# Second expert product with the weights stationary in five long lists, and a new way to preset the dispatch rows

## The chip, the cores and the metric

One core of one Trainium2 chip runs the whole program in one launch. The time is device microseconds (us) from the first to the last instruction of an execution. The kernel before takes 632.26 us, the median of 3 runs (632.22 to 633.16).

## What is computed

Three parts follow each other (reference, cut):

```python
# 1. attention: B=2, H=8, S=768, D=64, 16 clusters per head
mask = argmax(q_n @ c_n.T)[:, None] == argmax(k_n @ c_n.T)[None, :]
attn = softmax(where(mask, q @ k.T / 8, -1e9));  x = attn @ v      # 1536 tokens x 512
# 2. top-2 mixture of 8 experts, F=1024
out[tok] += w[tok] * (relu(x[tok] @ w1[e]) @ w2[e])                # per expert e
# 3. soft mixture: 8 experts x 4 slots, F=1024, softmax over tokens and over slots
```

## The kernel before, in words

**Attention.** The 16 heads are taken as 8 pairs p, each with two halves qh of the queries; I call the 16 steps h = 2p + qh *half-stages*. In one, TensorE (PE) computes six score tiles (`score`, L382 and L384), ScalarE (ACT) exponentiates them (L388), PE multiplies by v (`av`, L401), and GpSimd (POOL) adds up the exponentials (`add`, L418 and L421). Beside that PE finds the row maxima of the next half-stages (`munit`, L340, reduced by VectorE, DVE, L345 and L350). The finished maxima must become one row of the query operand (partition 96): `mfin` transposes them on DVE (L360) and writes the row with four DMAs (L363), except for the pairs in `TF`, where `mrow` does it with six small PE products (L371) and an ACT copy (L373). All loads go through one queue, SyncE's (SP), in the order of the program: for the next pair the values (`load_v`, L137) and the queries and keys (`load`, L128 and L129).

**Dispatch.** Each token's row (512 values and 4 of routing: expert, two weights, token number; `XR` = 516) is scattered to two of 3712 slots in DRAM (`xg`). Slots that stay empty must hold zeros and a token number that points to a row nobody reads (`TRASH` and above). `Dispatch.setup` (L498) makes constants on POOL and DVE at the end of half-stage 0 and presets the 4 routing columns of all slots with one DMA (L523); `fill` (L529) zeroes the other 512 columns of `xg`, and the sum of the experts `x2acc`, in 23 DMAs, four in each odd half-stage from h = 1.

**Experts.** The slots make ten jobs (lists) with 8 steps each, one step for 128 of the 1024 hidden units: two of 256 slots, six long ones of 448, 432, 408, 400, 392 and 384 used slots, and two of 240. Numbers are kept as the sum of a high and a low part (fp32r), so each product takes three matmuls. `first` (L1039) multiplies x by w1 with the weights stationary and the slots moving (L1054, 12 matmuls); ACT and DVE make the high and low part of the hidden row `H` (L1060, L1063). `second` (L1066) has it the other way round: H is stationary, 128 slots at a time, and the 512 columns of w2 move (L1095). A long list takes 9 such matmuls for its first 384 slots and, where there is a rest, 2 for the high and low part of the rest together: 11 of 512 columns, whatever the rest.

```python
for i, (a, x) in enumerate(((hi, XH), (hi, XL), (lo, XH))):     # first, four c each
    nc.tensor.matmul(ph[:, :u], a[:, 128 * c:128 * c + 128], x[:, c, :u], ...)
terms = [(py, HH[:, c], w, 0), (py, HH[:, c], v, 1), (py, HL[:, c], w, 2)]   # second
```

The order is written out: in step s come `first(s+1)`, `second(s)`, `split_hi(s+3)` on ACT (L952) and `split_lo(s+3)` on DVE (L959), which make the two parts of the weights in a ring of three, then pieces of the next list's x: `prep_t` (DVE transposes, L1009), `prep_h` (ACT), `prep_l` (POOL). After a list's last step `evac` weights the rows, and an indirect DMA of POOL adds them to `x2acc` (L1103). `xr` and `xT`, the two halves of one buffer, hold x before and after its transpose. `M2.load_w` loads the third part's weights, 2 MB at a time.

Of the kernel before, what the change touches and what calls it, by code (L numbers as in the profile page):

```python
# [472 lines left out]
class Dispatch:  # L473


    def __init__(self, tc, g, noise):
        self.tc, self.nc, self.g, self.noise_in = tc, tc.nc, g, noise
        xp = g.xp
        self.noise = xp.tile([128, NCK, E], F32, name="noise")
        self.z = g.place(DM)  # L480
        self.zm = g.place(NSL // 128, 4)
        g.xg = tc.dram_tile([NSL, XR], F32, name="xg")
# [15 lines left out]
    def setup(self):  # L498
# [16 lines left out]
        nc.gpsimd.tensor_tensor(self.lim, self.base, self.capm[:, None, :].to_broadcast([128, B, E]), op=OP.add)  # L515
        dv.tensor_scalar(self.lim[:, 1:, :NREG], self.lim[:, 1:, :NREG], float(LATE - RCAP), None, op0=OP.add)
# [10 lines left out]
        nc.gpsimd.tensor_copy(g.x[:, :, DM + 3], self.tok)  # L527

    def fill(self, i):  # L529

        nc, g = self.nc, self.g
        r = 2
        nx = NSL // 128
        for t, n in ((g.xg, nx), (g.x2, (NTOK + NTRASH) // 128)):
# [360 lines left out]
class MoE1:  # L895


    def __init__(self, tc, g, w12):
# [16 lines left out]
        self.wr, self.xr, self.xm, self.H, self.PH, self.PY = {}, {}, {}, {}, {}, {}  # L915
        self.scat = []
        self.spacer = mo.tile([1, 1], F32, name="spacer")
# [45 lines left out]
    def load_x(self, j):  # L963
# [7 lines left out]
        else:  # L971
            xg = lambda a, n, c: g.xg[r0 + a:r0 + a + n, c]
        xr, xT = self.XR[:, 0, x0:], self.XR[:, 1, x0:]
        for a in range(4):
# [49 lines left out]
    def prep_m(self, j):  # L1024

        nc, g = self.nc, self.g
        dv = nc.vector
        e, nb, xr, xT, xTv, mt, XH, XL, v = self.parts(j)
        del self.xr[j]
        k = mt.shape[1]  # L1030
        wt = g.mo0.tile([128, 4], F32, name="mwt", tag="mwt", bufs=2)[:, :k]
        di = g.mo0.tile([128, 4], U32, name="mdi", tag="mdi", bufs=2)[:, :k]
        dv.tensor_tensor(wt, mt[:, :, 1], mt[:, :, 2], op=OP.subtract)
        dv.scalar_tensor_tensor(wt, mt[:, :, 0], self.perm[:, j - NSRT:j - NSRT + 1] if e is None else float(e), wt, op0=OP.is_equal, op1=OP.mult)
        dv.tensor_tensor(wt, wt, mt[:, :, 2], op=OP.add)
        dv.tensor_copy(di, mt[:, :, 3])
        self.xm[j] = wt, di

    def first(self, s):  # L1039
# [17 lines left out]
        H = self.HT[:, s % 3]  # L1057
        m = n // 128 * 128
        HH, HL = H[:, :n], H[:, 2 * n - m:2 * n]
        nc.scalar.activation(HH[:, :u], ph[:, :u], AF.Relu)  # L1060
        for a, b, o in ((0, min(m, u), HL), (m, u, H[:, n:2 * n - m])):
            if a < b:
                nc.vector.scalar_tensor_tensor(o[:, :b - a], ph[:, a:b], 0.0, f32(HH)[:, a:b], op0=OP.max, op1=OP.subtract)  # L1063
        self.H[s] = HH, HL

    def second(self, s, ms=None):  # L1066
# [6 lines left out]
        hi, lo = self.ring[s]  # L1073
        last = j == len(self.jobs) - 1
        if f == NF - 1 and j not in self.Y:
            self.Y[j] = [self.mo.tile([128, DM], F32, name="y", tag="y", bufs=4) for i in range((n + 127) // 128)]
        nm = (n + 127) // 128
        for m in range(nm) if ms is None else ms:
# [7 lines left out]
            w, v = hi[:, 512:], lo[:, 512:]  # L1086
            if n - 128 * m >= 128:
                terms = [(py, HH[:, c], w, 0), (py, HH[:, c], v, 1), (py, HL[:, c], w, 2)]
            else:

                h = self.HT[:, s % 3, c.start:2 * n - c.start]
                o = py[:2 * (n - c.start)]
                terms = [(o, h, w, 0), (o, h, v, 2)]
            for o, x, y, i in terms:
                nc.tensor.matmul(o, x, y, start=(f == 0 and i == 0), stop=(f == NF - 1 and i == 2))  # L1095
            if f == NF - 1:
                for i in (m,) if last or m == nm - 1 and m % 2 == 0 else (m - 1, m) if m % 2 else ():
                    self.evac(j, i, self.PY[i])

    def add_rows(self, j, y, di, out):  # L1100
# [10 lines left out]
    def evac(self, j, m, py):  # L1111
# [3 lines left out]
        p = min(128, self.used[j] - 128 * m)  # L1115
        w = self.jobs[j][2] - 128 * m
# [3 lines left out]
        if w < 128:  # L1120
            nc.scalar.activation(yv, pv[w:w + p], AF.Copy, scale=wt[w:w + p, m:m + 1])
            for k in range(4):
                nc.vector.scalar_tensor_tensor(yv[:, k], pv[:p, k], wt[:p, m:m + 1],
                                               yv[:, k], op0=OP.mult, op1=OP.add)
        elif m % 2:
# [337 lines left out]
def body(tc, qk, q2, k2, v2, cent, wgn, noise, w12, phi, v12, out):  # L1463
    nc = tc.nc
    with ExitStack() as ctx:
# [103 lines left out]
        for n in range(1, NP):  # L1569
# [16 lines left out]
            at(post, 6 * h + (8 if n == 1 else 6), A.aql, n, 0)  # L1586
            at(post, 6 * h + 11, A.aql, n, 1)
            at(ends, h, A.load_v, n)
# [29 lines left out]
        for i in range(Dp.NFILL):  # L1618
            at(ends, 2 * (i // 4) + 1, Dp.fill, i)

# [85 lines left out]
        for h in range(2 * NP - 2):  # L1706
# [21 lines left out]
            for k in range(6):  # L1728
                A.av(p, 6 * qh + k)
                if s0 == 0 and k == 3:  # L1730
                    A.mrow(0, 1)
            gap(s0 + 5, 4)
            if s0 == 0:
                Dp.setup()
            run(ends, h)
# [49 lines left out]
        for s in range(ns):  # L1785
# [22 lines left out]
            if s == OV:  # L1808
                Dp.overflow(w12, lambda n: g.psum.tile([128, 512], F32, tag="mx", name=n, bufs=2))
                c_pre.close()  # L1810
                c_xp.close()
                M2.rooms(enter(c_w2, "m2w", side="right"), 6)
            q = s + 3
            soon = NREG * NF - 4 <= s < NREG * NF
# [5 lines left out]
            for fn, a in () if soon else prep.get(s, ()):  # L1820
                fn(*a)
            if s == 6:
                assert len(todo) <= 6
# [91 lines left out]
```

## Time and profile before

| | |
|---|---|
| median of 3 runs | 632.26 us |
| the profiled execution, its own time | 630.61 us |
| its span, first to last instruction | 628.8 us |
| PE busy | 605.9 us, 96% |
| DVE, ACT, POOL busy | 61%, 50%, 46% |
| granted PE clock | full in all 40 slices |

The profiled execution is 1.65 us below the median of the runs. A row of the timeline reads: start, duration, engine, line, operation, output<-inputs, shape, count, and in brackets the idle time before it with what ended it. A row of the chain of waits gives start, duration, engine, output and line; in it consecutive instructions of a line are one row.

### The profile page before, as it was taken

The numbers are of one execution on the slowest core, as the hardware profiler recorded it, in microseconds if no ns is written. First come the engines' busy times: TensorE is split into PE (matmuls) and PEld (weight loads), VectorE is DVE, ScalarE is ACT, GpSimd is POOL, SyncE is SP. The second block draws the span as 40 slices with busy tenths as digits, with TensorE's granted clock in tenths as the row PEclk, the third lists the DMA queues.
The fourth block names the chain that finished last, engine by engine and source line by source line (L and its number), as shares of the span: only waits on it lengthen the run. The fifth ranks groups of instructions, "written<-read, shape, count | busy, mean of one in ns | idle before, by whom it ended". The sixth has DMA issues, their size and how long they took to land. (4 is left out here: it accounts for less than half of the span.)

```text
span 628.8 us, 11424 instructions
## 1 busy us (share of the span) xinstructions
PE 605.9 (96%) x4169; PEld 472.5 (75%) x4169; DVE 385.0 (61%) x840; ACT 312.6 (50%) x444; POOL 287.1 (46%) x274
## 2 busy tenths in 40 slices
PE   8997999999999998999999999999999999988996
PEld 6665667666677667878888888888888888875544
DVE  6875667686776498757555445455544467646633
ACT  5857666676676661545344353444435445533002
POOL 3998777787989842642034241342513303120100
PEclk9999999999999999999999999999999999999999
DMA  8287474543446573897738559698794939988995
GB/s 327 68 188 211 182 267 169 212 151 124 142 178 211 203 208 124 281 237 194 168 100 181 164 203 254 233 299 311 234 334 140 235 128 342 296 255 302 427 388 201
DMA packets 62892, 139.50 MB, mean 222 GB/s; under 512 B 15280, under 2 KB 30832, under 8 KB 60784
## 3 DMA queue, kind: packets, MB, share of 16 engines
q1 hardware_dynamic: 56944, 125.31, 59.7%
q0 software_dynamic: 5888, 13.42, 9.9%
q8 instruction: 34, 0.56, 0.4%
q14 instruction: 26, 0.21, 0.1%
HBM read 108.18 MB, written 28.42 MB: 217 GB/s over the span
## 5 line engine op out<-in xcount | busy, mean ns | idle before, releaser
L1095 PE MATMUL py<-ring,H 128*128 128x512 f32 (+1 forms) x686 | 172.8, 396 | 1.2 <-DVE H L1063 1.2
L959 DVE TENSOR_TENSOR ring<-wr,ring 128x1024 fp32r<-128x1024 f32 (+1 forms) x77 | 95.0, 1235 | 103.6 <-ACT ring L952 103.5
L1095 PEld LDWEIGHTS py<-ring,H 128*128 128x128 f32 (+1 forms) x686 | 123.7, 184 | 28.4 <-DVE H L1063 2.5
L952 ACT ACTIVATE ring<-wr 128x1024 fp32r<-128x1024 f32 x77 | 81.6, 1061 | 92.0 <-PE py L1095 82.3
L1103 POOL DMA_INDIRECT x2acc<-y,mdi x31 | 50.4, 1625 | 103.5 <-ACT y L1128 97.7
L345 DVE TENSOR_REDUCE mp<-pmx 128x1 f32<-128x512 f32 x96 | 63.6, 683 | 15.8 <-PE pmx L340 15.4
L1060 ACT ACTIVATE H<-ph 128x256 fp32r<-128x256 f32 (+7 forms) x80 | 36.7, 459 | 67.7 <-PE ph L1054 61.6
L388 ACT ACTIVATE pts<-psc 128x768 f32<-128x768 f32 x72 | 57.8, 812 | 25.2 <-PE psc L384 20.2
L1054 PE MATMUL ph<-XS1a,ring 128*128 128x240 f32 (+3 forms) x288 | 67.8, 325 | 0.0
L1054 PE MATMUL ph<-XS0a,ring 128*128 128x432 f32 (+3 forms) x252 | 63.1, 332 | 0.9 <-DVE dt L448 0.7
L1063 DVE SCALAR_TENSOR_TENSOR H<-ph,H 128x384 fp32r<-128x384 f32 (+2 forms) x120 | 43.4, 389 | 18.9 <-ACT H L1060 18.0
L421 POOL TENSOR_TENSOR psa<-psa,pts 128x768 f32<-128x768 f32 x27 | 49.8, 1845 | 4.7 <-ACT pts L388 3.0
L401 PE MATMUL pav<-pts,vt 128*64 128x384 f32 x288 | 51.7, 492 | 0.0
L1054 PEld LDWEIGHTS ph<-XS1a,ring 128*128 128x128 f32 x288 | 47.7, 188 | 3.6 <-DVE ring L959 0.2
L1054 PE MATMUL ph<-XS0b,ring 128*128 128x256 f32 (+3 forms) x192 | 46.7, 316 | 1.4 <-ACT ring L952 0.8
L1054 PE MATMUL ph<-XS1b,ring 128*128 128x240 f32 (+3 forms) x192 | 46.1, 313 | 0.8 <-DVE ring L959 0.8
L1022 POOL TENSOR_TENSOR XS0b<-xr,XS0a 128x512 fp32r<-128x512 f32 (+1 forms) x9 | 16.8, 1869 | 64.7 <-ACT XS0a L1016 64.7
L1054 PEld LDWEIGHTS ph<-XS0a,ring 128*128 128x128 f32 x252 | 43.3, 189 | 3.7 <-DVE dt L448 0.9
L382 PE MATMUL psc<-oddb 97*128 97x384 f32 x96 | 34.0, 354 | 3.6 <-ACT pts L388 2.1
L401 PEld LDWEIGHTS pav<-pts,vt 128*64 128x64 f32 x288 | 19.2, 136 | 23.3 <-issue 21.5
L757 POOL DMA_INDIRECT xg<-x,idx x24 | 25.8, 1075 | 21.4 <-DVE inv L690 15.5
L350 DVE TENSOR_REDUCE mp<-pmx 128x2 f32<-128x512 f32 x48 | 33.0, 687 | 3.2 <-PE pmx L340 2.6
(373 smaller groups left out, 1048.3 us busy)
## 6 DMA issues: line engine op xcount, KB each, us to landing
wr<-in_w SPq DMA_DIRECT2D x80, 512.0 KB
v<-in_v SPq DMA_DIRECT2D x9, 2048.0 KB
xg<-xr SPq DMA_DIRECT2D x14, 512.0 KB
wr<-in_qk SPq DMA_DIRECT2D x8, 768.0 KB
early<-in_q SPq DMA_DIRECT2D x8, 768.0 KB
early<-in_k SPq DMA_DIRECT2D x8, 768.0 KB
x2acc<-xr SPq DMA_DIRECT2D x8, 512.0 KB
vt<-in_v SPq DMA_DIRECT2D x8, 384.0 KB
```

The source lines that it names most:

```text
L345: nc.vector.tensor_reduce(mp[:, 0, col:col + 1], ps, axis=AX.X, op=OP.max)
L382: nc.tensor.matmul(ps[:, hh, :384], self.BK[i][:97, hh, ks], self.BQ[i][:97, qh, hh], start=True, stop=False)
L388: nc.scalar.activation(pt, ps[:, :, :384], AF.Exp, scale=SCALE)
L401: nc.tensor.matmul(self.avp[p, qh][64 * hh:64 * hh + 64, :384], self.vt[p][:, hh, kc, :], pt[:, hh, :], start=(kc == 0), stop=(kc == 5))
L421: eng.tensor_tensor(s, s, pt.pop((p, t)), op=OP.add)
L952: self.nc.scalar.activation(self.ring[s][0], self.wr[s], AF.Copy)
L959: nc.vector.tensor_tensor(lo[:, :n], wr[:, :n], f32(hi)[:, :n], op=OP.subtract)
L1054: nc.tensor.matmul(ph[:, :u], a[:, 128 * c:128 * c + 128], x[:, c, :u], start=(c == 0 and i == 0), stop=(c == 3 and i == 2))
L1060: nc.scalar.activation(HH[:, :u], ph[:, :u], AF.Relu)
L1063: nc.vector.scalar_tensor_tensor(o[:, :b - a], ph[:, a:b], 0.0, f32(HH)[:, a:b], op0=OP.max, op1=OP.subtract)
L1095: nc.tensor.matmul(o, x, y, start=(f == 0 and i == 0), stop=(f == NF - 1 and i == 2))
L1103: st = nc.gpsimd.indirect_dma_start(out=out, out_offset=bass.IndirectOffsetOnAxis(ap=di, axis=0), in_=y, in_offset=None, compute_op=OP.add)
```

## The change

1. In the five long lists whose length is no multiple of 128 (448, 432, 408, 400, 392) `second_t` takes the place of `second`: w2 is stationary, 128 of its 512 columns at a time, and H moves with the used width u: 12 matmuls a step. The result is transposed, so at the end ACT copies it to a buffer T, DVE transposes it back in 16 pieces of 32 partitions during the next list's first five steps (`TURN`), and ACT weights the rows in its sixth step, followed by the four scatter-adds. T is the second half of the x buffer (x is now transposed in place), and the rows go to two buffers by turns: one of the pool and a room of the third part's weights, whose load moves from step 52 to step 58.
2. The DMA of the routing columns is gone: a fill of `xg` writes whole rows of 516 from a row that holds zeros and the trash number. `Dispatch.setup` moves to the end of half-stage 3, its DVE part to half-stage 4, and the fills start at h = 3.
3. The maxima row of pair 1, half 0 is made by `mrow` (PE and ACT) and no longer by DVE and four DMAs.
4. `H` keeps its low part in one piece, so DVE makes it with one instruction where there were two.

```diff
-TF = (0, 0), (0, 1)
+TF = (0, 0), (0, 1), (1, 0)
+V1 = 32, 36, 40, 44, 48, 58
+TURN = 3, 4, 3, 3, 3, 4, 0, 0
...
-        nc.gpsimd.memset(self.zm, 0.0)
-        for n in range(0, NSL // 128, 4):
-            m = min(4, NSL // 128 - n)
-            io(self.zm[:, n:n + m, 3], [[128, m]], TRASH, 1)
-        nc.sync.dma_start(g.xg[:, DM:].rearrange("(n p) d -> p n d", p=128), self.zm)
+        io(self.z[:, DM + 3:], [[0, 1]], TRASH, 1)
...
-                nc.sync.dma_start(t[256 * i:256 * i + 128 * m, :DM].rearrange("(n p) d -> p n d", p=128),
-                                  self.z[:, None, :].to_broadcast([128, m, DM]))
+                nc.sync.dma_start(t[256 * i:256 * i + 128 * m].rearrange("(n p) d -> p n d", p=128),
+                                  self.z[:, None, :w].to_broadcast([128, m, w]))
...
-        for a, b, o in ((0, min(m, u), HL), (m, u, H[:, n:2 * n - m])):
-            if a < b:
-                nc.vector.scalar_tensor_tensor(o[:, :b - a], ph[:, a:b], 0.0, f32(HH)[:, a:b], op0=OP.max, op1=OP.subtract)
+        nc.vector.scalar_tensor_tensor(HL[:, :u], ph[:, :u], 0.0, f32(HH)[:, :u], op0=OP.max, op1=OP.subtract)
...
+        if self.used[j] % 128 and not self.short[j]:
+            self.second_t(s)
+            return
...
+    def second_t(self, s):
+        nb = n // 32
+        if f == NF - 1:
+            T = self.XR[:, 1].rearrange("p (m b c t) -> p m b c t", m=4, b=4, t=32)
+            Tv = T.rearrange("p m b c t -> p (m b) c t")
+        for c in range(4):
+            py = self.PY[c]
+            k = slice(512 + 128 * c, 640 + 128 * c)
+            for i, (a, x) in enumerate(((hi, HH), (hi, HL), (lo, HH))):
+                w = n if f == 0 and i == 0 else u
+                nc.tensor.matmul(py[:, :w], a[:, k], x[:, :w], start=(f == 0 and i == 0), stop=(f == NF - 1 and i == 2))
+            for d in (c - 1, c) if f == NF - 1 and c % 2 else ():
+                nc.scalar.activation(Tv[:, :nb, d], self.PY[d][:, :n].rearrange("p (b t) -> p b t", t=32), AF.Copy)
+            def turn(a, b):
+                k = (nb - b + 3) // 4
+                nc.vector.transpose(Y[32 * b:32 * b + 32, :k, 128 * a:128 * a + 128],
+                                    T[32 * a:32 * a + 32, :k, b].rearrange("p m c t -> p m (c t)"))
+            def rows(m):
+                p = min(128, u - 128 * m)
+                nc.scalar.activation(Y[:p, m], Y[:p, m], AF.Copy, scale=wt[:p, m:m + 1])
+                self.add_rows(j, Y[:p, m], di[:p, m:m + 1], g.x2)
...
-            at(ends, 2 * (i // 4) + 1, Dp.fill, i)
+            at(ends, 2 * (i // 4) + 3, Dp.fill, i)
...
-            if s0 == 0:
-                Dp.setup()
+            if h in (3, 4):
+                (Dp.setup if h == 3 else Dp.setup2)()
...
-            if s >= 4 * NF and s % 4 == 0:
+            if s in V1:
                 M2.load_w()
```

On PE, in the list of 408 slots, one step before (`ph` is the first product, `py` the second, XS1a and XS1b the parts of x, `ring` the weights):

```order
926 L1054 MATMUL ph<-XS1a,ring 128x408
927 L1095 MATMUL py<-ring,H 128x512 x9
928 L1095 MATMUL py<-ring,H 64x512 x2
929 L1054 MATMUL ph<-XS1a,ring 128x408
930 L1054 MATMUL ph<-XS1b,ring 128x408
```

and the same step now:

```order
970 L1054 MATMUL ph<-XS1b,ring 128x408
971 L1054 MATMUL ph<-XS1a,ring 128x408
972 L1121 MATMUL py<-H,ring 128x408 x12
973 L1054 MATMUL ph<-XS1a,ring 128x408
974 L1054 MATMUL ph<-XS1b,ring 128x408
```

The place in the order is the same; eleven matmuls of 512 columns have become twelve of 408.

On SP, the queue of the loads, at the end of half-stage 0 and in half-stage 1 before (`xr` is the constants' place, `early` the raw queries and keys of pair 2, `vt` the values of pair 1, `nmt` the transposed maxima):

```order
15 L133 DMA wr<-in_qk 128x1536
16 L503 DMA noise<-in_noise 128x96
17 L523 DMA xg<-xr 128x29x4
18 L137 DMA vt<-in_v 128x768
19 L128 DMA early<-in_q 128x1536
20 L129 DMA early<-in_k 128x1536
21 L363 DMA oddb<-nmt 1x6x32 x4
```

and now:

```order
15 L135 DMA wr<-in_qk 128x1536
16 L139 DMA vt<-in_v 128x768
17 L130 DMA early<-in_q 128x1536
18 L131 DMA early<-in_k 128x1536
19 L290 DMA even<-xr 16x384 x2
```

The noise, the routing columns and the four DMAs of the maxima row no longer stand in this stretch.

On DVE, the first two steps of the list of 392 slots now (`v_3784` is the room of the third part's weights, here the buffer of the turned rows of the list of 400; L1033 to L1036 are `prep_m`, the row weights of the new list; L1060 is the low part of H, L959 `split_lo`):

```order
595 L959 TENSOR_TENSOR ring<-wr,ring 128x1024
596 L1033 TENSOR_TENSOR mwt<-mt 128x4
597 L1034 SCALAR_TENSOR_TENSOR mwt<-mt,perm,mwt 128x4
598 L1035 TENSOR_TENSOR mwt<-mwt,mt 128x4
599 L1036 CAST mdi<-mt 128x4
600 L1130 STREAM_TRANSPOSE v_3784<-xr 32x4x128 x3
601 L1060 SCALAR_TENSOR_TENSOR H<-ph,H 128x392
602 L959 TENSOR_TENSOR ring<-wr,ring 128x1024
603 L1130 STREAM_TRANSPOSE v_3784<-xr 32x4x128
604 L1130 STREAM_TRANSPOSE v_3784<-xr 32x3x128 x3
```

Before, these steps had two L1063 instructions in the place of each L1060 and no L1130: three and four transposes stand ahead of the next low part of H.

## Rows read from the trace of the kernel before

**Rows 1.** The page's part 1: busy time, share of the span, instructions of each engine.

```profile
PE 605.9 (96%) x4169; PEld 472.5 (75%) x4169; DVE 385.0 (61%) x840; ACT 312.6 (50%) x444; POOL 287.1 (46%) x274
```

**Rows 2.** The chain of waits, expert stage: start, us, engine, output, line, count.

```profile
342.28 2.35 PE ph L1054 x12
...
366.88 2.22 PE ph L1054 x12
...
405.07 2.16 PE ph L1054 x12
...
442.94 2.12 PE ph L1054 x12
445.06 2.57 PE py L1095 x11
...
532.01 1.34 PE ph L1054 x12
```

**Rows 3.** Timeline of PE, one step of the list of 448.

```profile
296.87 0.36 PE L1054 MATMUL ph<-XS1a,ring 128*128 128x448 f32 x1
...
299.30 2.73 PE L1095 MATMUL py<-ring,H 128*128 128x512 f32 x11
301.87 0.36 PE L1054 MATMUL ph<-XS1a,ring 128*128 128x448 f32 x1
```

**Rows 4.** Who waited for whom, PE, 0 to 60 us: total, times, longest.

```profile
PE psc L382 <- ACT pts L388: 2.1, 1, 2.1
PE psc L382 <- DMA oddb<-nmt: 1.5, 1, 1.5
```

**Rows 5.** Timeline of SP, half-stages 0 and 1.

```profile
34.09 0.40 SPq L523 DMA_DIRECT2D xg<-xr  x1
...
36.89 0.43 SPq L129 DMA_DIRECT2D early<-in_k  x1
```

**Rows 6.** DMA of 30 to 52 us, all queues.

```profile
DMA packets 4850, 3.23 MB, mean 147 GB/s; under 512 B 4112, under 2 KB 4336, under 8 KB 4848
```

**Rows 7.** Timeline of ACT, end of half-stage 1.

```profile
49.59 0.85 ACT L301 ACTIVATE even<-early 64x768 fp32r<-64x768 f32 x1 [6.62 <-DMA early<-in_k]
```

**Rows 8.** Timeline of PE, the maxima row of pair 0, half 1.

```profile
30.94 0.52 PE L371 MATMUL pnm<-odda,nm 128*1 128x128 f32 x6
31.38 1.51 PE L401 MATMUL pav<-pts,vt 128*64 128x384 f32 x8
```

**Rows 9.** DVE by line and shape: total busy us, mean ns, idle before.

```profile
L959 DVE TENSOR_TENSOR ring<-wr,ring 128x1024 fp32r<-128x1024 f32 x74 | 92.0, 1244 | 98.2 <-ACT ring L952 98.1
...
L1063 DVE SCALAR_TENSOR_TENSOR H<-ph,H 128x384 fp32r<-128x384 f32 x48 | 26.4, 551 | 14.5 <-ACT H L1060 14.0
L1009 DVE STREAM_TRANSPOSE xr<-xr 128x512 f32<-128x512 f32 x18 | 12.6, 703 | 3.2 <-DMA xr<-xg 1.9 <-DMA ident_i<-in_phi 1.3
...
L226 DVE STREAM_TRANSPOSE xr<-psim 128x384 f32<-128x384 f32 x8 | 4.6, 577 | 0.8 <-PE psim L223 0.5
```

**Rows 10.** Busy time of each engine over the list of 392, with clock and DMA.

```profile
443.00:480.00 37.00, 37.00 (x183) 32.27 (x182) 18.93 (x36) 15.92 (x22) 11.66 (x11) 1.00 0.85 267
```

**Rows 11.** Timeline of POOL, the setup, and half-stage 3 to 4.

```profile
31.07 0.13 POOL L501 IOTA iode<- 128x8 f32 x1
...
34.00 0.21 POOL L527 COPY x<-tok 128x12 f32<-128x12 f32 x1
...
77.59 1.83 POOL L312 TENSOR_TENSOR odda<-early,oddb 64x768 fp32r<-64x768 f32 x1
81.60 1.84 POOL L418 TENSOR_TENSOR psa<-pts 128x768 f32<-128x768 f32 x1 [2.17 <-ACT pts L388]
```

**Rows 12.** Timeline of SP, the last pair's weights.

```profile
211.13 0.84 SPq L948 DMA_DIRECT2D wr<-in_w  x2
```

**Rows 13.** Timeline of ACT, the last pair.

```profile
216.69 2.01 ACT L952 ACTIVATE ring<-wr 128x1024 fp32r<-128x1024 f32 x2
```

**Rows 14.** Timeline of DVE, the last pair.

```profile
224.83 2.87 DVE L959 TENSOR_TENSOR more<-wr,more 128x1024 fp32r<-128x1024 f32 x1
```

More of the change, by code (lines that the diff above doesn't have):

```diff
@@ L479, in __init__ @@
         self.noise = xp.tile([128, NCK, E], F32, name="noise")
-        self.z = g.place(DM)
-        self.zm = g.place(NSL // 128, 4)
+        self.z = g.place(XR)
         g.xg = tc.dram_tile([NSL, XR], F32, name="xg")
@@ L533, in fill @@
         nx = NSL // 128
-        for t, n in ((g.xg, nx), (g.x2, (NTOK + NTRASH) // 128)):
+        for t, n, w in ((g.xg, nx, XR), (g.x2, (NTOK + NTRASH) // 128, DM)):
             if i < (n + r - 1) // r:
                 m = min(r, n - r * i)
-                nc.sync.dma_start(t[256 * i:256 * i + 128 * m, :DM].rearrange("(n p) d -> p n d", p=128),
-                                  self.z[:, None, :].to_broadcast([128, m, DM]))
+                nc.sync.dma_start(t[256 * i:256 * i + 128 * m].rearrange("(n p) d -> p n d", p=128),
+                                  self.z[:, None, :w].to_broadcast([128, m, w]))
                 return
@@ L915, in __init__ @@
         self.wr, self.xr, self.xm, self.H, self.PH, self.PY = {}, {}, {}, {}, {}, {}
-        self.scat = []
+        self.scat, self.turns = [], []
         self.spacer = mo.tile([1, 1], F32, name="spacer")
@@ L972, in load_x @@
             xg = lambda a, n, c: g.xg[r0 + a:r0 + a + n, c]
-        xr, xT = self.XR[:, 0, x0:], self.XR[:, 1, x0:]
+        xr = xT = self.XR[:, 0, x0:]
         for a in range(4):
@@ L1030, in prep_m @@
         k = mt.shape[1]
-        wt = g.mo0.tile([128, 4], F32, name="mwt", tag="mwt", bufs=2)[:, :k]
-        di = g.mo0.tile([128, 4], U32, name="mdi", tag="mdi", bufs=2)[:, :k]
+        wt = g.mo0.tile([128, 4], F32, name="mwt", tag="mwt", bufs=3)[:, :k]
+        di = g.mo0.tile([128, 4], U32, name="mdi", tag="mdi", bufs=3)[:, :k]
         dv.tensor_tensor(wt, mt[:, :, 1], mt[:, :, 2], op=OP.subtract)
@@ L1057, in first @@
         H = self.HT[:, s % 3]
[L1058 to L1059 removed]
+        HH, HL = H[:, :n], H[:, CAP:CAP + n]
         nc.scalar.activation(HH[:, :u], ph[:, :u], AF.Relu)
[L1061 to L1063 removed]
+        nc.vector.scalar_tensor_tensor(HL[:, :u], ph[:, :u], 0.0, f32(HH)[:, :u], op0=OP.max, op1=OP.subtract)
         self.H[s] = HH, HL
@@ L1074, in second @@
         last = j == len(self.jobs) - 1
+        if self.used[j] % 128 and not self.short[j]:
+            self.second_t(s)
+            return
         if f == NF - 1 and j not in self.Y:
-            self.Y[j] = [self.mo.tile([128, DM], F32, name="y", tag="y", bufs=4) for i in range((n + 127) // 128)]
+            if not self.short[j]:
+                y = self.XR[:, 1].rearrange("p (m d) -> p m d", d=DM)
+            elif j % 2 == 0:
+                y = self.y4 = self.rows4()
+            else:
+                y = self.y4[:, 2:]
+            self.Y[j] = [y[:, i] for i in range(n // 128)]
         nm = (n + 127) // 128
@@ L1086, in second @@
             w, v = hi[:, 512:], lo[:, 512:]
[L1087 to L1095, printed above, removed]
+            for i, (x, y) in enumerate(((HH[:, c], w), (HH[:, c], v), (HL[:, c], w))):
+                nc.tensor.matmul(py, x, y, start=(f == 0 and i == 0), stop=(f == NF - 1 and i == 2))
             if f == NF - 1:
@@ L1098, in second, with rows4 @@
                     self.evac(j, i, self.PY[i])
+    def rows4(self):
+        return self.mo.tile([128, 4, DM], F32, name="y", tag="y")
+    def second_t(self, s):
+        nc, g = self.nc, self.g
+        j, f = self.steps[s]
+        n, u = self.jobs[j][2], self.used[j]
+        HH, HL = self.H.pop(s)
+        hi, lo = self.ring[s]
+        nb = n // 32
[3 more added lines that the diff above has]
+        for c in range(4):
+            if f == 0 and c % 2 == 0:
+                two = g.psum.tile([128, 2, 512], F32, tag="sc", name="py", bufs=2)
+                self.PY[c], self.PY[c + 1] = two[:, 0], two[:, 1]
+            py = self.PY[c]
[5 more added lines that the diff above has]
+                nc.scalar.activation(Tv[:, :nb, d], self.PY[d][:, :n].rearrange("p (b t) -> p b t", t=32), AF.Copy)
+        if f == NF - 1:
+            Y = self.wide if j % 2 else self.rows4()
+            wt, di = self.xm[j]
+            def turn(a, b):
[6 more added lines that the diff above has]
+                self.add_rows(j, Y[:p, m], di[:p, m:m + 1], g.x2)
+            self.turns = [lambda a=a, b=b: turn(a, b) for b in range(4) for a in range(4)]
+            self.turns += [lambda m=m: rows(m) for m in range((n + 127) // 128)]
     def add_rows(self, j, y, di, out):
@@ L1119, in evac @@
         pv = py.rearrange("p (k a j) -> p k a j", a=4, k=4)
[L1120 to L1125, printed above, removed]
+        if m % 2:
             nc.vector.tensor_scalar(yv, pv[:p], wt[:p, m:m + 1], None, op0=OP.mult)
@@ L1586, in body @@
             at(post, 6 * h + (8 if n == 1 else 6), A.aql, n, 0)
-            at(post, 6 * h + 11, A.aql, n, 1)
+            at(post, 6 * h + (12 if n == 1 else 11), A.aql, n, 1)
             at(ends, h, A.load_v, n)
@@ L1729, in body @@
                 A.av(p, 6 * qh + k)
-                if s0 == 0 and k == 3:
-                    A.mrow(0, 1)
+                if divmod(h + 1, 2) in TF and k == 3:
+                    A.mrow(*divmod(h + 1, 2))
             gap(s0 + 5, 4)
-            if s0 == 0:
-                Dp.setup()
+            if h in (3, 4):
+                (Dp.setup if h == 3 else Dp.setup2)()
             run(ends, h)
@@ L1812, in body @@
                 M2.rooms(enter(c_w2, "m2w", side="right"), 6)
+                M1.wide = M2.free[5][:, :4 * DM].rearrange("p (m d) -> p m d", d=DM)
             q = s + 3
@@ L1821, in body @@
                 fn(*a)
+            for i in range(TURN[f] if j > NREG else 0):
+                if M1.turns:
+                    M1.turns.pop(0)()
             if s == 6:
```

7 lines of the change are left out of this document (4 added, 3 removed).

## The prediction, made before the changed kernel ran

> **What bounds the kernel now.** I read the page's busy times first: PE is busy for 605.9 of 628.8 us [rows 1], so what PE doesn't have to do, and what it doesn't wait for, is what counts. The chain of waits says where: through the five long lists it consists of PE alone, first product and second product by turns, without a wait between them [rows 2], and the windows agree: over the list of 392 PE is busy for all of 37 us, DVE for 18.93, ACT for 15.92, the DMA engines for 0.85 of the time, at a granted clock of 1.00 [rows 10]. There every column that PE need not stream is time. The list of PE's waits then shows two of the longest that it has in the attention part, both between half-stage 1 and half-stage 2: 1.5 us for the DMAs of the maxima row and 2.1 us for an exponential [rows 4]. The rest of the program hardly touches the change.
>
> **The second product.** Before, a step of a long list has 11 second matmuls in 2.57 us [rows 2], 233 ns for 512 columns. The new ones have the shape of the first product of the same list: weights of 128x128 from the ring, u columns moving, 12 of them. So their price is on the same rows: 2.35 us for 432 columns, 2.22 for 408, 2.16 for 400, 2.12 for 392 [rows 2], and for 448 the distance of the first matmul to the second product, 299.30 - 296.87 = 2.43 [rows 3]. (The last distance, 301.87 - 299.30, is 2.57 again, so the price of 11 holds in each list.) The saving of a step is 0.14, 0.22, 0.35, 0.41 and 0.45 us, together 1.57; times 8 steps that is 12.6. In the first step of a list four of the twelve are up to 24 columns wider; at about 0.46 ns a column, (2.43 - 2.12) / 12 / 56, this is under 0.05 us a list. I take **12.3 us**, all of it on the path, since PE waits for nothing there.
>
> The Trainium skill speaks against this. Its page "TensorE: Matmul & The Clock Gate", section "Back-to-back issue gap", gives a sustained spacing of 81 ns for 128 columns and 131 ns for 512; by a straight line between them 12 matmuls of 448 take about 1.47 us and 11 of 512 take 1.44, and over the five lists the change would save an estimated 0.8 us and not 12.3. This trace disagrees: its 512 columns take 233 ns.
>
> What lies beside PE must stay beside it. DVE gets 16 transposes a list. A row of 512 elements on 128 partitions takes 703 ns and one of 384 takes 577 [rows 9]; that these have 32 partitions I count as no gain, which leaves 8 x 0.70 + 8 x 0.58 = 10.2 us for a list of 14 blocks of 32 slots. At the other end, an instruction of `split_lo` that takes 1.24 us on the mean [rows 9] took 2.87 beside POOL [rows 14], 2.3 times as long; that bounds a transpose at 1.6 us. I take 0.7, since nothing like that stretch's POOL work stands in the lists. DVE then has at most 18.9 + 10.2 = 29 us of 34 a list. In the crowded steps a weight split of 1.24, a low part of H of some 0.6 (0.55 for 384 columns [rows 9]), a `prep_t` of 0.70 and three transposes of 0.58 make about 4.3 us, against a step of 4.24 (2 x 2.12). DVE runs full there, falls behind by some tenths, and has the three steps without transposes to recover. It may: ACT splits a step's weights in 1.0 [rows 13] from the end of a second product on, DVE in 1.24 more, and PE reads them 4.24 later, a slack of about 2 us. I charge 0.3. ACT gets four copies at a list's end and four weightings in the sixth step in place of three evacuations, with 15.92 of 37 us busy: nothing. The scatter-adds come six steps later; only the next list's row buffer waits for them. The 2 MB load that moves from step 52 to 58 lowers the traffic of the lists where steps get shorter and adds it to the list of 384; I charge 0.1.
>
> **The start of the attention.** The DMA of the routing columns is issued at 34.09, ahead of the next pair's values, queries and keys, whose last is issued at 36.89 [rows 5]; in 30 to 52 us 4112 of 4850 packets are under 512 B, and the mean is 147 GB/s [rows 6]. ACT stands still for 6.62 us until the keys land at 49.59 [rows 7], three more copies stand ahead of its next exponential, and that is PE's wait of 2.1. The wait of 1.5 is for the maxima row, whose four DMAs stand in the same queue behind these. Without the small packets the keys stand with 2.7 MB in the queue; at 314 GB/s, the 267 of rows 10 divided by their share of 0.85, that takes 8.6 us from about 32 on. They are there by about 42 (an estimate), before ACT asks for them. Both waits go: **3.6 us**. The maxima row costs PE six small matmuls, 31.38 - 30.94 = 0.44 us [rows 8], and ACT a copy in time that it has. ACT makes it behind the copy that needs the keys; should these be late, the row is late too.
>
> **What is moved.** The setup's small instructions take POOL at most 3.1 us, from 31.07 to 34.21, of which the routing columns' part goes. They now stand ahead of the subtraction that starts at 77.59; the addition behind that waits 2.17 us for ACT until 81.60 [rows 11], and this gap hides most of them. If it closed, the additions would come 1 to 3 us late, and seven buffers of exponentials stand between these and PE. The DVE part is four small instructions, once. Fills, still four a time, end two half-stages later, so three of them (1.5 MB) now stand in SP's queue ahead of the weights issued at 211.13 [rows 12]. At 314 GB/s the fills and the first weights, 2.1 MB, take 6.7 us from 211 on, and start and landing come on top: about 219.5. ACT splits them as the second of two from 216.69 on, so wants them at 217.7 [rows 13]. It would be about 2 us late, PE has two score buffers in hand, and I charge 0.4. Together new waits: 0.3 + 0.1 + 0.4 = **0.8 us**.
>
> **Sum.** 12.3 + 3.6 - 0.4 - 0.8 = 14.7 us. The profiled execution took 630.61, its copy would take 615.9. The runs' median lies 1.65 above that execution, so I set the sum against 632.26 and forecast **617.6 us**.
>
> **Rivals.** (a) *The attention waits return elsewhere*: the keys are late all the same, or the fills before the last pair's weights cost PE their whole 2 us. Then 12.3 remains with up to 1 of the 3.2: 619 to 621. Against it stands the DMA time that is gone. 0.13. (b) *DVE or the weights' loads hold up PE in the lists*, by 0.3 to 0.6 us in each of the 25 steps with transposes: 8 to 15 us, 625 to 632. For it: DVE's 4.3 of 4.24 us, and 0.85 of the DMA time already taken [rows 10]; against it the slack of 2 us and three free steps. A smaller part of this, 2 to 5 us, is likelier: 619.5 to 622.5. Together 0.10. (c) *The other side: PE's pace goes by matmuls, not by columns.* If a matmul took 2.57 / 11 = 0.234 us at any width, 12 would take 2.80, and 40 steps would lose 0.23 each, 9.4 us: 632.3 + 9.4 - 2.4 = 639. It decides from 0.219 us a matmul on, where the lists lose the 2.4 that the attention gains. Against it: the first product's matmuls take 2.43 / 12 = 0.20 us at 448 columns and 1.34 / 12 = 0.11 us at 240 [rows 2, 3]. 0.02. A pace as flat as this is what the Trainium skill's figures, above, come near. (d) *Transposes at their upper bound*: at 1.6 us a list's DVE time is 18.9 + 25.6 = 44.5 us against PE's 8 x (2.57 + 2.26) = 38.6 now, the lists become DVE's, and five of them lose 29: about 659. It turns slower at about 1.26 us apiece, (38.6 + 0.5 - 18.9) / 16, the 0.5 being a fifth of the attention's 2.4. 0.02. (e) *The change doesn't do what it says*: a part of the 12 stays wide. The order of PE shows 12 of width u in each step, so this is in none of my numbers.
>
> **Chances and range.** The forecast's own case, 616 to 619, has 0.70; 0.03 goes to times below, when waits of PE on DVE in these stretches vanish too. The range takes in (a) and the lesser part of (b): **614.5 to 622.0 us**. A measurement here tells about 0.2% from no change, 1.3 us. Faster has (a), the forecast, what is below and nearly all of (b), 0.95; slower has (c) and (d), 0.04; the same has the end of (b), 0.01.
>
> **What would show it.** In the new profile the chain should show 12 second matmuls in 2.43, 2.35, 2.22, 2.16 and 2.12 us, PE without idle time in the lists, and the step from 448 to 392 shrinking from 4.86 to 4.24. PE's two waits at 47 to 53 us should be gone, the keys of pair 2 should land before 43, and six more L373 matmuls stand in half-stage 1. A transpose of 32 partitions near 0.6 to 0.7 us bears out the DVE sum. The forecast is wrong if PE waits for `ring` or `H` in the lists (then (b)), if the new matmuls stay near 233 ns (then (c)), or if ACT waits for `wr` or `early` in the attention part (then (a)).

## The result, and the profile after

The changed kernel takes **624.5 us** (median of 4 runs, 621.9 to 627.2), where the kernel before takes 632.7 beside it: a ratio of 0.9871, 95% interval 0.9839 to 0.9903, so 8.2 us less. The forecast was 617.6 with a range of 614.5 to 622.0. The direction holds, the time lies outside the range, and 6.5 of the 14.7 us forecast did not come. The profiled execution of the changed kernel took 622.3, with a span of 620.5; that of before had 628.8.

Line numbers have moved. The second product of the long lists is L1121, its transposes back are L1130, low part of H L1060, weight split on DVE L959 (as before), `prep_t` L1009 (as before), loads of the next list's rows L975, 2 MB load L1205, maxima row L373. In the kernels of the experiments lines may shift by two.

Part 1 of the page, which answers to [rows 1]: PE has 7.8 us less to do, DVE 41 us more.

```profile
PE 598.1 (96%) x4215; PEld 482.7 (78%) x4215; DVE 426.2 (69%) x854; ACT 323.0 (52%) x470; POOL 288.3 (46%) x266
```

The chain of waits (start, us, what) from the last second product of 408 columns (401.00) into the list of 392, to set beside [rows 2]:

```profile
401.00 2.21 PE py L1121 x12
...
436.90 2.17 PE py L1121 x12
439.07 2.13 PE ph L1054 x12
441.20 2.19 PE py L1121 x12
443.39 2.13 PE ph L1054 x12
445.53 2.14 PE py L1121 x12
...
456.20 2.14 PE ph L1054 x12
458.34 0.56 DVE v L1130
458.90 0.01 issue
458.91 0.57 DVE v L1130
459.48 0.01 issue
459.49 0.57 DVE v L1130
460.06 0.03 issue
460.09 0.58 DVE H L1060
460.67 0.04 issue
460.71 3.42 PE py L1121 x11
```

Two things stand in these rows. The 12 new matmuls take about what the forecast said: 2.21 us at 408 columns, 2.17 at 400 (436.90), 2.14 at 392 (445.53) and 2.19 in the first step of 392 (441.20), where four of the twelve are wider. And in the middle of the list PE isn't in the chain for 2.4 us: three transposes of 0.57 us and the low part of H are, one behind the other on DVE. Behind them one second product takes 3.42 us in place of 2.14. The list of PE's waits in the five lists has this and two smaller ones (total, times, longest):

```profile
PE py L1121 <- DVE H L1060: 3.0, 3, 2.2
```

The timeline of DVE shows what stood ahead of the three transposes; the last row is the same wait in the kernel before:

```profile
453.03 1.22 DVE L959 TENSOR_TENSOR ring<-wr,ring 128x1024 fp32r<-128x1024 f32 x1
457.58 0.71 DVE L1009 STREAM_TRANSPOSE xr<-xr 128x512 f32<-128x512 f32 x1 [3.34 <-DMA xr<-xg]
458.32 1.74 DVE L1130 STREAM_TRANSPOSE v<-xr 32x384 f32<-32x384 f32 x3
460.09 0.57 DVE L1060 SCALAR_TENSOR_TENSOR H<-ph,H 128x392 fp32r<-128x392 f32 x1
```
```profile
464.92 0.71 DVE L1009 STREAM_TRANSPOSE xr<-xr 128x512 f32<-128x512 f32 x1 [1.10 <-DMA xr<-xg]
```

DVE was idle for 3.34 us, because `prep_t` is next in its order and the next list's rows had not landed. The transposes need none of these rows, nor does H, but they stand behind. The Trainium skill, page "Perfetto Trace Analysis", section "Tensor Engine Instruction (MATMUL, LD_WEIGHTS)", calls DVE, ACT and GpSimd strict FIFOs; these rows agree for DVE. The timeline of SP suggests why the rows were late: the 2 MB load is issued ahead of them, and the four loads of the rows take 5.91 us to issue (4.61 in the kernel before). Experiment 11 tests this.

```profile
437.44 0.45 SPq L1205 DMA_DIRECT2D v<-in_v  x1
442.27 0.33 SPq L946 DMA_DIRECT2D wr<-in_w  x1
442.83 5.91 SPq L975 DMA_DIRECT2D xr<-xg  x4
449.01 0.40 SPq L987 DMA_DIRECT2D mt<-xg  x1
```

Busy times by stretch (us; PE, PEld, DVE, ACT, POOL; granted clock; DMA share; GB/s), to set beside [rows 10]:

```profile
436.00:440.00 4.00, 4.00 (x25) 4.00 (x24) 1.61 (x2) 2.32 (x6) 3.46 (x5) 1.00 1.07 195
...
452.00:456.00 4.00, 4.00 (x24) 4.00 (x23) 2.21 (x3) 1.34 (x2) 0.00 (x0) 1.00 1.20 189
456.00:460.00 4.00, 2.51 (x15) 2.18 (x13) 2.36 (x4) 2.08 (x3) 0.96 (x1) 1.00 0.84 280
460.00:464.00 4.00, 3.29 (x12) 3.29 (x13) 3.91 (x7) 0.10 (x1) 0.30 (x1) 0.67 0.32 105
```

The DMA engines are taken from 436 to 456, with a share of 1.00 or more in each stretch of 4 us (0.85 on the mean of this list in the kernel before). After PE's idle time its granted clock is 0.67 of full in the next 4 us, a mixture of the two levels, 1.2 and 2.4 GHz.

In the attention part both waits of [rows 4] are gone: PE is busy for 7.96 of the 8 us from 44 to 52, and the DMA engines, which sent small packets there before, have nothing left to do at the end. The prediction's 2.7 MB had mostly gone by 40 us, where the traffic falls from 403 to 49 GB/s.

```profile
36.00:40.00 4.00, 4.00 (x23) 3.36 (x22) 3.49 (x6) 3.57 (x6) 3.84 (x3) 1.00 0.97 403
40.00:44.00 4.00, 3.90 (x56) 2.03 (x57) 3.78 (x10) 3.77 (x5) 3.84 (x3) 1.00 0.21 49
44.00:46.00 2.00, 2.00 (x18) 0.92 (x16) 1.64 (x2) 1.33 (x3) 0.94 (x2) 1.00 0.61 160
46.00:48.00 2.00, 2.00 (x15) 1.22 (x12) 0.00 (x0) 1.35 (x3) 1.93 (x2) 1.00 0.68 283
48.00:52.00 4.00, 3.96 (x23) 3.20 (x22) 3.22 (x7) 2.82 (x5) 2.22 (x2) 1.00 0.00 0
```

**The account.** I set marks in the timeline of PE at the first matmul of 448 columns and at the first of 384, which is behind the list of 392. For the kernel before and the changed one:

```profile
289.44 0.36 PE L1054 MATMUL ph<-XS1a,ring 128*128 128x448 f32 x1
...
480.30 0.33 PE L1054 MATMUL ph<-XS0a,ring 128*128 128x384 f32 x1
```
```profile
287.08 0.36 PE L1054 MATMUL ph<-XS1a,ring 128*128 128x448 f32 x1
...
472.86 0.34 PE L1054 MATMUL ph<-XS0a,ring 128*128 128x384 f32 x1
```

| stretch, us | before | changed | difference | forecast |
|---|---|---|---|---|
| up to the first 448 | 289.44 | 287.08 | -2.4 | -2.8 |
| 448 to 432 | 37.47 | 36.85 | -0.6 | -1.0 |
| 432 to 408 | 39.81 | 38.29 | -1.5 | -1.7 |
| 408 to 400 | 38.19 | 36.44 | -1.8 | -2.7 |
| 400 to 392 | 37.87 | 35.95 | -1.9 | -3.2 |
| 392 to 384 | 37.52 | 38.25 | +0.7 | -3.6 |
| the five stretches | 190.85 | 185.78 | -5.1 | -12.1 |
| from there on | 148.53 | 147.67 | -0.9 | -0.45 |

(A first product is issued ahead of the last second product of the list before, so a stretch has one second product of the old width and seven of its own. The forecast column is the prediction's saving of a step taken so; its 0.4 of new waits in the lists is left out.) So 7.0 us are missing in the five lists, 4.3 of them in the last.

In the two lists before the last one something else adds to DVE's time. A weight split, 1.2 us otherwise, took 2.13 and 2.12 us in the list of 408 and 2.01 in that of 400, each beside a subtraction of POOL:

```profile
427.31 2.01 DVE L959 TENSOR_TENSOR ring<-wr,ring 128x1024 fp32r<-128x1024 f32 x1
```
```profile
426.95 1.30 POOL L1022 TENSOR_TENSOR XS1b<-xr,XS1a 128x512 fp32r<-128x512 f32 x1 [3.63 <-ACT XS1a L1016]
```

PE's wait of 0.47 us in the list of 400 comes one step later. In the five lists of the kernel before and of experiment 4 below no split takes over 1.35 us. The prediction counted 1.24 us for each split in the lists; how much of the 1.7 us that these two lists take more than in experiment 4 is due to this was not measured apart.

### The profile page after: what moved, and what is told of

It is laid out like the page before. It is cut to its first block, busy times and chain, and to the rows that moved or that the text cites. A ratio compares the mean times of both kernels' runs of the same rounds, so it can differ in the third digit from the quotient of the medians.

```text
span 620.5 us, 11580 instructions
## 1 busy us (share of the span) xinstructions
PE 598.1 (96%) x4215; PEld 482.7 (78%) x4215; DVE 426.2 (69%) x854; ACT 323.0 (52%) x470; POOL 288.3 (46%) x266
## 5 line engine op out<-in xcount | busy, mean ns | idle before, releaser
L959 DVE TENSOR_TENSOR ring<-wr,ring 128x1024 fp32r<-128x1024 f32 (+1 forms) x77 | 98.6, 1281 | 64.6 <-ACT ring L952 64.5
L1121 PE MATMUL py<-H,ring 128*128 128x448 f32 (+5 forms) x480 | 100.1, 356 | 3.0 <-DVE H L1060 3.0
L1121 PEld LDWEIGHTS py<-H,ring 128*128 128x128 f32 x480 | 89.2, 190 | 7.2 <-DVE H L1060 4.6
L1094 PE MATMUL py<-ring,H 128*128 128x512 f32 x246 | 63.7, 397 | 1.2 <-DVE H L1060 1.2
L1144 POOL DMA_INDIRECT x2acc<-y,mdi x20 | 32.8, 1640 | 60.3 <-ACT y L1135 24.8
L1060 DVE SCALAR_TENSOR_TENSOR H<-ph,H 128x256 fp32r<-128x256 f32 (+7 forms) x80 | 41.0, 513 | 18.0 <-ACT H L1059 16.8
L1094 PEld LDWEIGHTS py<-ring,H 128*128 128x128 f32 x246 | 43.9, 188 | 10.2 <-DVE H L1060 2.5
L1022 POOL TENSOR_TENSOR XS0b<-xr,XS0a 128x512 fp32r<-128x512 f32 (+1 forms) x9 | 14.8, 1646 | 76.4 <-ACT XS0a L1016 76.4
```

The source lines that it names most:

```text
L959: nc.vector.tensor_tensor(lo[:, :n], wr[:, :n], f32(hi)[:, :n], op=OP.subtract)
L1060: nc.vector.scalar_tensor_tensor(HL[:, :u], ph[:, :u], 0.0, f32(HH)[:, :u], op0=OP.max, op1=OP.subtract)
L1094: nc.tensor.matmul(py, x, y, start=(f == 0 and i == 0), stop=(f == NF - 1 and i == 2))
L1121: nc.tensor.matmul(py[:, :w], a[:, k], x[:, :w], start=(f == 0 and i == 0), stop=(f == NF - 1 and i == 2))
L1144: st = nc.gpsimd.indirect_dma_start(out=out, out_offset=bass.IndirectOffsetOnAxis(ap=di, axis=0), in_=y, in_offset=None, compute_op=OP.add)
```

## The experiments

The theory: DVE works in order and waits for the next list's rows, with the transposes of the second product and the low part of H behind that wait; PE runs out of H, and loses clock on top. Its rivals: DVE has too much work, whatever it waits for; the parts of the change disturb each other; the rows' later treatment would help any kernel. Experiments 1 to 4 ran beside a kernel before of 631.0 us, 5 to 8 beside 637.6, 9 to 12 beside 638.9, so ratios are compared, and the five stretches (the same marks as above), which the first 287 us and the tail don't touch. Much of what differs between the groups lies outside the lists: in experiments 4 and 12, the same kernel, the lists begin at 287.67 and 292.96 us, and both spend 180.33 in the stretches.

| | ratio to before, 95% | five stretches, us |
|---|---|---|
| the kernel before | 1 | 190.85 |
| the change (first result; again in 5) | 0.987 (0.984 to 0.990); 0.988 (0.985 to 0.991) | 185.78; 187.41 |
| 1 lists alone | 0.994 (0.992 to 0.997) | 189.35 |
| 2 attention alone | 0.997 (0.995 to 0.998) | 190.87 |
| 3 rows loaded earlier | 0.982 (0.979 to 0.985) | 181.55 |
| 4 rows transposed later; again in 12 | 0.979 (0.976 to 0.982); 0.983 (0.980 to 0.986) | 180.33; 180.33 |
| 6 lists alone, rows later | 0.989 (0.985 to 0.992) | 180.33 |
| 7 rows later, no transposes back | 0.978 (0.976 to 0.981) | 180.11 |
| 8 before, rows later | 1.000 (0.998 to 1.002) | 190.85 |
| 9 the change, no transposes back | 0.982 (0.979 to 0.985) | 180.05 |
| 10 transposes back first | 1.036 (1.033 to 1.039) | 208.03 |
| 11 2 MB loads two steps later | 0.980 (0.977 to 0.984) | 180.07 |

**1 and 2: the change in two halves.** In 1 the hunks of the attention part, `setup`, `fill` and `TF` are as before; in 2 only these are changed.

> The five long lists, the in-place rows and the moved 2 MB load as in the change; the attention part, its setup and its fills as before. If the loss against the forecast lies in the lists (theory), this gains about 5 to 6.5 us on the kernel before, where the forecast's own terms for this part (12.3 less 0.4) say 11.9: about 626.5 and not 620.5. PE should wait for H some 2 us in one of the last two long lists, as in the change. If the attention part and the lists disturb each other (rival: moved fills and setup cost it), this alone gains 8 or more.

> The attention part alone: token-wide fills two half-stages later, setup in the fourth half-stage, one more maxima row by TensorE; lists as before. Forecast's terms for this part: 3.6 - 0.44 - 0.4 = 2.8 us less than before, 629.5. The traces of the two kernels have the first product start 2.3 us earlier, so the theory expects 2.0 to 2.5, about 630.0, with both waits of PE at 47 to 53 us gone. The rival that the moved work costs something later in the attention gives under 1.5.

The lists alone gave 628.3 against 631.0, by the ratio 3.6 us (1.9 to 5.4 by the interval) and not 11.9; the theory's 5 to 6.5 was high too. The attention alone gave 2.0 us (1.2 to 2.9 by the interval), so its part of the forecast, 2.8, stands within what can be told, and the loss lies in the lists. The two halves together, 5.6 us by their ratios, give less than the change's 8.2, so nothing points at a loss from putting them together. In 1 the waits are longer than in the change; PE's waits, and then DVE's in the list of 392:

```profile
PE py L1123 <- DVE H L1062: 5.4, 3, 4.4
```
```profile
461.21 0.71 DVE L1011 STREAM_TRANSPOSE xr<-xr 128x512 f32<-128x512 f32 x1 [5.51 <-DMA xr<-xg]
```

**3 and 4: the rows in time, by two ways.** The load a step earlier, or the transposes a step later:

```diff
-            if 2 <= j < 8 and f == 1:
+            if 2 <= j < 8 and f == (1 if j == 2 else 0):
                 M1.load_x(j + 1)
```
```diff
-PREP = {2: (12, 2, "dd"), 4: (2, 3, "ppp"), ...
+PREP = {2: (12, 2, "dd"), 4: (3, 2, "pp"), ...
```

> The change, with the loads of the next list's rows issued one step earlier (step 0 of a list, ahead of the 2 MB load); DVE's work is the same. Theory: DVE, which works in order, waits for these rows (1.3 and 3.3 us in the last two long lists), and three transposes and the low part of H stand behind that wait; without it PE's 2.2 us wait for H and the fall of the clock behind it go: 3 to 5 us less than the change, 618 to 621, and runs that agree better. Rival: DVE has too much work in these steps whatever the rows do: less than 1 us of gain, 622 to 627 as before the edit.

> The change, with the transposes of the next list's rows on DVE one step later and in two parts in place of three (steps 3 and 4, their high parts in 4 and 5, their low parts in 5 and 6); the loads stay where they are. Theory (DVE waits for the rows): as with the earlier load, 618 to 621. Rival (DVE's amount of work): less than 1 us, or slower, since two larger parts make the crowded steps fuller.

Both came as the theory had it, the second by 0.3 us below its range: 619.0 and 617.7 against 631.0. DVE has no less to do in either, so the rival of its amount of work falls. In 3 PE still waits for H twice, 1.0 us together, in the lists of 408 and 400, and the stretches take 1.2 us more than in 4: there DVE waits 1.84 and 2.08 us for ACT's part of the weights, and transposes and H stand behind that wait. In 4 the row of DVE at the same place has no wait:

```profile
456.32 1.23 DVE L959 TENSOR_TENSOR ring<-wr,ring 128x1024 fp32r<-128x1024 f32 x1 [0.53 <-ACT ring L952]
457.47 0.97 DVE L1009 STREAM_TRANSPOSE xr<-xr 128x768 f32<-128x768 f32 x1
458.47 0.57 DVE L1130 STREAM_TRANSPOSE v<-xr 32x384 f32<-32x384 f32 x1
```

and of PE's waits from 287 to 470 us one remains. It is at 286.64 us, ahead of the first long list, and the kernel before has it too (0.47 us at 288.43); inside the five long lists PE waits no more:

```profile
PE py L1094 <- DVE H L1060: 0.5, 1, 0.5
```

**5 to 8: the same, by halves, and without the transposes.** 5 is the change again. 6 is experiment 1 with the edit of experiment 4. 7 is experiment 4 with this edit:

```diff
-            self.turns = [lambda a=a, b=b: turn(a, b) for b in range(4) for a in range(4)]
+            self.turns = [lambda: None] * 16
...
-                nc.scalar.activation(Y[:p, m], Y[:p, m], AF.Copy, scale=wt[:p, m:m + 1])
+                nc.scalar.activation(Y[:p, m], T[:p, min(m, 2)].rearrange("p b c t -> p (b c t)"), AF.Copy, scale=wt[:p, m:m + 1])
```

> The change itself once more, beside the kernels below on the same chip: by its ratio of 0.987, 622 to 625 where the kernel before takes 631 to 632.

> The lists alone (attention part as before), with the later transposes of the rows of the earlier experiment. If DVE's wait for the rows is what ate the lists' gain (theory), this shows the forecast's own term for the lists, 12.3 less some 1.5 that the lists still lose with the later transposes: 10 to 11.5 us less than before, about 620.5. Rival: the lists alone gained 3.6, and the later transposes bring it no more than the 5 us that they brought the change: 622.5 or above.

> The change with the later transposes of the rows, and without the 16 transposes a list that turn the second product back into token rows: what is scattered is a scaled copy that is not turned (and for the last block a copy of the third), so the output is another. DVE has 10 us less work a list. Theory (the amount of DVE's work costs little once it no longer waits for the rows): at most 1 us less than with the later transposes alone, 616.5 to 618. Rival (DVE is full): 2 us less or more.

> The kernel before, with the later transposes of the rows alone. There DVE's wait for the rows has neither transposes nor a late part of H behind it that PE wants, so theory expects no change: within 1 us of before. If the later transposes were a gain by themselves, in whatever kernel, this shows 3 us or more.

5 repeated the ratio, at 629.5 us beside 637.6 (622 to 625 was expected beside 631 to 632); here DVE waited up to 4.8 us for the rows and PE 3.7 for H, and the stretches came out at 187.41: the size of the stall changes from execution to execution. 6 gave 7.1 us by its ratio (4.9 to 9.3), short of the 10 to 11.5 expected; but its five stretches are those of experiment 4 to the hundredth, 10.5 us less than before, so in that execution the lists give what the theory said, while the median of the whole times shows less of it. Its runs spread from 626.2 to 632.7, and the profiled one is the fastest of them. 7 gained nothing that can be measured on experiment 4, and 0.22 us in the stretches: the 80 transposes, 49 us of DVE, cost 0.2 us once DVE doesn't wait. 8 changed nothing, so the later transposes are no gain of their own.

**9 to 12: what it takes.** 9 is the change with the edit of 7, and the rows as late as ever. 10 puts a step's `turns` ahead of its `prep`, 11 moves the 2 MB loads, 12 is experiment 4 again.

```diff
-V1 = 32, 36, 40, 44, 48, 58
+V1 = 34, 38, 42, 46, 50, 58
```

> The change without the 16 transposes a list that turn the second product back (scattered is a scaled copy that is not turned, so the output is another); the transposes of the next list's rows stay at step 2, where they wait for their DMA. Theory: it takes both, the wait and the 1.74 us of transposes behind it: without these the low part of H comes 1.7 us earlier, PE's wait shrinks from 2.2 us to 0.5 or less, and this gains 3 to 5 us on the change, a ratio to before of 0.979 to 0.983. Rival: the wait alone is enough to hold PE up: less than 1.5 us gained, 0.986 or above.

> The change with a step's transposes of the second product ahead of the transposes of the next list's rows on DVE, in place of behind them; the work is the same. Theory: the 1.74 us then run while the rows are still under way, DVE's wait of 3.3 us shrinks by as much, and PE's wait for H nearly goes: 3 to 5 us less than the change, 0.979 to 0.983. Rival (DVE's amount of work): no change, 0.987.

> The change with the five 2 MB loads two steps later (steps 2 and 6 of a list in place of 0 and 4), so that none is issued in the step before the next list's rows. If the 2 MB load ahead of them is what makes the rows late (theory), they land some 6 us earlier, before DVE asks, and this gains 3 to 5 us on the change: 0.979 to 0.983. Rival: the rows are late because of the weights and scatters in the same stretch: less than 1.5 us, 0.985 or above.

> The change with the later transposes of the rows once more, beside the three above on the same chip: its ratio to before was 0.979; 0.977 to 0.981 expected.

9 settles how the loss comes about. DVE waits for the rows much as in the change (3.34 us there in the list of 392; the end of the first wait is put down to `mt`, which is loaded behind the rows),

```profile
426.99 0.71 DVE L1009 STREAM_TRANSPOSE xr<-xr 128x512 f32<-128x512 f32 x1 [2.31 <-DMA mt<-xg]
462.01 0.71 DVE L1009 STREAM_TRANSPOSE xr<-xr 128x512 f32<-128x512 f32 x1 [2.89 <-DMA xr<-xg]
```

and PE doesn't feel it: 180.05 us. So neither a wait of up to 2.9 us alone costs anything (9), nor the transposes alone (4), and both together cost 5.5 us in the change's profile and 7.1 in experiment 5. 11 shows why the rows are late: with the 2 MB load two steps further on, their issue takes 2.35 us in place of 5.91, DVE waits for none of them, and the stretches take 180.07.

```profile
449.10 2.35 SPq L975 DMA_DIRECT2D xr<-xg  x4
```

10 missed, by over 30 us, and for a reason that is none of the theories'. `turns` also holds the four weightings of the rows and their scatter-adds, and my edit put those of step 5, the sixth, ahead of POOL's part of the next list's x. POOL works in order too (timeline of POOL; idle time and its end in brackets):

```profile
410.78 1.80 POOL L1144 DMA_INDIRECT x2acc<-v,mdi  x1 [2.94 <-ACT v L1135]
...
417.34 1.39 POOL L1144 DMA_INDIRECT x2acc<-v,mdi  x1 [0.26 <-issue]
418.27 2.03 POOL L1022 TENSOR_TENSOR XS0b<-xr,XS0a 128x640 fp32r<-128x640 f32 x1
```
```profile
420.35 0.70 PE L1054 MATMUL ph<-XS0b,ring 128*128 128x400 f32 x1 [6.78 <-POOL XS0b L1022]
```

The low part of x, which PE needs at 413.57, comes at 420.35. There are three such waits in 10, of 6.8 to 6.9 us, one a list. Transposes first with the scatters behind was not tried, so 10 says nothing sure about DVE's order: DVE waits for no rows in it, but these stalls also give the rows time. It shows the same trap on a second engine: where in the order a thing stands, not how much there is.

Experiments 4 and 11 beat both kernels: their ratios to before are 0.979 and 0.983 (4, twice; the second, 12, lies above its 0.977 to 0.981, and its interval reaches into that of the change) and 0.980 (11), the change's 0.987 and 0.988, and their stretches 180.33, 180.33 and 180.07 us against 185.78 and 187.41.

## Why the prediction was wrong

- **The second product: right in price.** "2.35 us for 432 columns, 2.22 for 408, 2.16 for 400, 2.12 for 392" came as 2.35 to 2.36, 2.24 to 2.27, 2.15 to 2.18 and 2.13 to 2.16 in experiment 11, where PE doesn't wait for H; in the change 448 columns took 2.47 (294.41 - 291.94) and not 2.43. With the stall away, the five stretches give 10.8 of 12.1 us (experiments 9 and 11; 10.5 in 4). By the starts of the products in experiment 11, eight steps of 448 at 0.04 to 0.05 us over the price and eight of 408 at 0.02 to 0.05 over it make about 0.6 of the missing 1.3 us, and the wider first steps, which the forecast column leaves out, up to 0.25 by the prediction's own figure; the rest was not traced.
- **The step that failed:** "DVE runs full there, falls behind by some tenths, and has the three steps without transposes to recover ... a slack of about 2 us ... I charge 0.3." The amount of work was counted well: a transpose takes 0.70 and 0.57 us, said were 0.70 and 0.58, and all of them together cost 0.2 us (7 against 4). What the count left out was the split beside POOL, above. The step's error is that it left out that DVE also *waits*, at a place ahead of this work. The row was on the table: [rows 9] has `prep_t` with 3.2 us of idle time before it, ended by DMAs. In the kernel before the low part of H follows that wait too (465.56, right behind the 1.10 us), and PE doesn't wait for it. The change put 1.74 us of transposes between, and the wait grew in the list of 392 from 1.10 us to 3.34: counted from the list's first matmul (442.78 before, 434.61 now), DVE asks for the rows 1.4 us earlier, since the steps are shorter, and the rows come 0.8 later. Wait, transposes and H together use up the slack (experiments 4, 9 and 11). In place of 0.3 us the lists lost 5.5 in this execution (185.78 - 180.33), 7.1 in experiment 5 and 9.0 in experiment 1.
- **Rival (b)** had the place ("PE waits for `ring` or `H` in the lists") and a price of 2 to 5 or 8 to 15 us; the 7.0 us that are missing lie between the two. But its reason was DVE's load of 4.3 us in 4.24. That isn't the mechanism: with the same load and the rows in time (4) PE waits nowhere in the five lists. Its other reason, the DMA time already taken, comes nearer, but it spoke of the weights' loads and not of the next list's rows.
- **The attention part: within what can be told.** Both waits went. ACT first reads the keys of pair 2 at 43.37, without a wait, where before it waited for them until 49.59 [rows 7]; the DMA traffic above fits the estimate of 42. Of 2.8 us, 2.0 (alone) to 2.4 (in the change) arrived. The sign of rival (a), ACT waiting for `wr`, did show: 2.65 us before 217.79, for the last pair's weights behind the moved fills, where the prediction said about 2. It cost little: ahead of it ACT is 2.66 us earlier than before (211.89 - 209.23), and the lists begin 2.36 earlier.
- **Rival (c) and (d): excluded.** 448 columns take 2.47 / 12 = 206 ns and 392 take 178, so PE's pace goes by columns; a transpose takes 0.57 or 0.70 us and not 1.6. The Trainium skill's page "TensorE: Matmul & The Clock Gate", section "Back-to-back issue gap", by which the lists would save an estimated 0.8 us, doesn't fit: they saved 10.8 with the rows in time.
- **The sum of the account:** -2.36 - 5.07 - 0.86 = -8.29 us, the difference of the two spans. With the rows in time it is 628.8 - 615.9 = 12.9 (experiment 4), against 14.7.

## What to carry to other kernels

When work is put on an engine that isn't the bottleneck, look first for the waits that this engine already has, idle or not, and see what the new work stands behind and what stands behind it: a wait that costs nothing is cheap only as long as what follows it still comes in time. A full engine and a waiting one are different risks, and a load's due time has to be set against the shorter steps that the change makes. When part of a gain is missing, take it apart by stretches: a stretch that repeats to the hundredth over executions tells more than whole times that spread by several us.

## What the runs showed of the hardware

**The clock made long waits of PE dearer than they were long.** In the change PE's wait of 2.2 us was followed by 4 us at 0.67; in experiment 1, 4.4 us by stretches of 0.67 and 0.50; in experiment 10, 6.78 us by 0.50, the lower level, with matmuls of 400 columns about 0.33 us apart in place of 0.18. Against experiment 4 the list of 392 took 3.8 us more for 2.2 of waiting in the change, 5.1 for 3.7 in experiment 5, 7.1 for 4.4 in experiment 1: PE has no other wait in this list, and what is left beside it, 1.4 to 2.7 us, I put down to the clock: the product right behind the wait took 3.42 us in the change in place of 2.14. No run changes the clock alone. The Trainium skill, page "TensorE: Matmul & The Clock Gate", section "HAM oscillation — how this bites in real kernels", describes clock loss after waits for DMAs; these rows show the same, here after a wait for another engine.

**The tail has such a place too.** PE waits there for the sum of the experts on its way back from DRAM. In the change that wait is 1.3 us and the clock stays full; in experiment 11 it is 3.7. The busy times of the same 12 us, of the change and of experiment 11, and PE's wait in the latter, from its timeline:

```profile
561.00:573.00 12.00, 9.36 (x152) 6.25 (x150) 7.09 (x37) 4.54 (x12) 0.00 (x0) 1.00 0.97 351
```
```profile
563.00:575.00 12.00, 7.65 (x69) 5.53 (x68) 4.43 (x20) 1.65 (x4) 0.00 (x0) 0.72 0.85 290
```
```profile
569.15 1.97 PE L1290 MATMUL pt<-ident,XS1ab 128*128 128x128 f32 x8 [3.68 <-DMA XS1ab<-x2acc]
```

From the last mark on, 11 takes 151.75 us and the change 147.67. Of the 5.7 us by which 11 is faster in the lists, 4.1 go there. Over the traces of all runs but 10 the part behind that mark grows with the wait, whatever the kernel: 147.6 to 148.5 us with a wait of 0.8 to 1.3, 149.0 to 150.1 with 1.6 to 2.3, 150.2 with 2.6 to 2.7, 151.8 with 3.7. Experiments 4 and 12, the same kernel, stand at both ends of it, with 147.9 and 150.2. Why the sum comes back later in some executions, and whether the change's own runs of 622 and 627 differ by this, stays open.
